# Two tiles of the second chunk run inside the first chunk's tail, and start-up work is spread over other steps

## The chip, the cores and the metric

The kernel runs on one core of one Trainium2 chip. The metric is the device time of one execution in microseconds (us). Three runs gave 989.15, 988.88 and 988.53 us, so the median is 988.88. The engines are named as the profile names them: PE does matrix multiplication (PEld is its weight load), DVE is the vector engine, ACT the scalar engine, POOL is GpSimd, and SP only issues transfers.

## The reference

The input `x` has 8 batches of 3136 rows of 256 numbers. The result is the real part of a two-dimensional Fourier transform of each batch, followed by a layer norm, a two-layer network with a ReLU, and a residual sum.

```python
X = np.fft.fft(x, axis=1); X = np.fft.fft(X, axis=2); x = X.real
mu, var = mean(x), mean((x - mu) ** 2)             # over the last axis, 256
xn = (x - mu) / np.sqrt(var + 1e-06) * g_ln
out = x + np.maximum(xn @ w_ch1, 0.0) @ w_ch2      # 256 -> 1024 -> 256
```

## The kernel before, in words

**Stages.** The transform over 3136 rows is done in two steps. Step 1 (`step1`, pieces `i` 0 to 6 of a batch) is a 64-point transform; its result goes to a buffer in DRAM (`store1`) and comes back in another layout (`relayout`). Step 2 (`step2(m, part)`, 64 pieces) finishes the rows: it makes some 196 tokens per piece in PSUM (part `m`), and copies them out three ways: `f` the full value `ck` (ACT), `h` the value rounded to fp32r `ck_hi` (ACT), `l` the rest `ck_lo` (DVE). A token stands for a row and its mirror row. 256 tokens are a chunk `c`; a piece of step 2 can end one chunk and begin the next. Tiles of `ck`, `ck_hi` and `ck_lo` have three buffers, so chunk 3 takes the buffer of chunk 0.

**The network.** The transform over 256 columns is folded into `w1` at the start. Each chunk has 8 tiles `f` of 128 of the 1024 hidden units. `moe1_a(s)` is 6 matmuls into `ab` (two PSUM buffers), which ACT copies (`asb`) and DVE adds and subtracts (`h`, two instructions); `moe1_b(s)` is the ReLU (`h_hi`, ACT) and the rounding rest (`h_lo`, DVE); `moe2(s)` is 12 matmuls with `w2_hi` and `w2_lo` that add to `acc[c, i]`. `residual(c, i)` makes x itself on PE (`psy`), `residual_e` (ACT) and `residual_y` (DVE) finish it and take its statistics, `std` and `inverse_std` make the factor of the layer norm, and `finish` and `store_out` end the chunk. `psy` of chunk c lies in the PSUM buffers that `acc` of chunk c+1 uses next.

**The order.** Nothing schedules the work on PE, ACT, DVE and POOL: they run it in the order in which it is written. After a prologue the main loop takes one step `s` per tile: `moe1_b(s - 1)`, `moe1_a(s)`, then what `add_late` put at `s`, `moe2(s - 3)`, then what `add` put at `s`. Before the change, step `s` is tile `f = s % 8` of chunk `s // 8`.

**Weights.** They arrive as 64-bit floats and are converted in pieces of 512 columns: `convert_z` (ACT) and `convert_m`, `convert_b` (DVE, two instructions each) take a number apart, `finish_w2` (DVE) joins it, `split_w2` rounds it on ACT (`w2_hi`) and takes the rest on POOL (`w2_lo`). Piece `n` of `w2` serves tiles f = 2n and 2n + 1. `rest_w1` and `rest_w1_copy` give `w1_lo`; its second half serves tiles f = 4 to 7. At the start of step 2 PE runs ten matmuls on zeros (`warm_up`).

Of the kernel before, what the change touches and what calls it, by code (L numbers as in the profile page):

```python
# [32 lines left out]
CW = 256  # L33
# [113 lines left out]
def tile_kernel(ctx: ExitStack, tc: tile.TileContext, x, g_ln, w1, w2, tu, tab, tz, ty, tw, out):  # L147
# [121 lines left out]
    def store1(b, i, eng=nc.sync):  # L269
        s = s1[b][:, 2 * i:2 * i + 2]  # L270
        in_order(eng.dma_start(scratch[b][2 * i:2 * i + 2].rearrange("s p d -> p s d"),
                               s.rearrange("p a h d -> p a (h d)")))
# [11 lines left out]
    def width(c):  # L284
        return MAXW if c == LC else CW

    def first_token(m):
        b, j = divmod(m, 8)
        return b * REG + max(gb[2 * j] - 2, 0)
# [49 lines left out]
    PASSES = ((0, 1), (1, 0), (0, 0))  # L339
    hh = {}  # L340

    def moe1_a(s, passes=((0, 1), (1, 0), (0, 0))):
        c, f = divmod(s, 8)
        w = width(c)
        ch = chunk[c][1:]
        fs = slice(128 * f, 128 * f + 128)
        wt = (w1_hi, w1_lo)
        if w <= CW:
            ab = psum.tile([128, 2, CW], F32, tag="ab", name=f"ab{s}", bufs=2)
            pa, pb = ab[:, 0], ab[:, 1]  # L350
        else:
            pa = psum.tile([128, MAXW], F32, tag="ab", name=f"aa{s}", bufs=2)
            pb = psum.tile([128, MAXW], F32, tag="fft", name=f"bb{s}")
        for j, pt in ((0, pa), (1, pb)):
            for n, (wi, xi) in enumerate(passes):
                nc.tensor.matmul(pt, wt[wi][:, j, fs], ch[xi][:, j, :w],  # L356
                                 start=(n == 0), stop=(n == 2))
        asb = work.tile([128, MAXW], F32, tag="asb", name=f"asb{s}")
        h = hh[s] = work.tile([128, 2 * CW], F32, tag="h", name=f"h{s}", bufs=4)
        m = 2 * CW - w  # L360
        nc.scalar.copy(asb[:, :w], pa)  # L361
        nc.vector.tensor_tensor(out=h[:, :w], in0=asb[:, :w], in1=pb, op=ALU.add)  # L362
        nc.vector.tensor_tensor(out=h[:, w:], in0=asb[:, :m], in1=pb[:, :m], op=ALU.subtract)  # L363
# [21 lines left out]
    def in_order(dma):  # L385

        if main:
            tc.keep_in_program_order(dma)
# [6 lines left out]

    def moe2(s, halves=((0, 0), (0, 1), (1, 0), (1, 1))):

        c, f = divmod(s, 8)
        hs = hh[s]
        ws = (w2_hi, w2_lo)  # L400
        for i, side in halves:
            if f == 0 and side == 0:
                acc[c, i] = psum.tile([128, 2, D], F32, tag=f"acc{c % 2}", name=f"acc{c}_{i}", bufs=2)
            h0 = 256 * i + 128 * side if c == LC else 128 * i + 256 * side
            for n, (wi, xi) in enumerate(PASSES):
                nc.tensor.matmul(acc[c, i][:, side], hs[xi][:, h0:h0 + 128], ws[wi][:, f],  # L406
                                 start=(f == 0 and side == 0 and n == 0),
                                 stop=(f == 7 and n == 2), skip_group_check=True)
# [93 lines left out]
    def convert_a(key, wp):  # L502
        convert_m(key, wp)
        convert_z(key, wp)
# [10 lines left out]
    def convert_m(key, wp):  # L515

        high, e = conv[key] if key in conv else convert_e(key, wp)
        low = wp.bitcast(U32).rearrange("p (n two) -> p n two", two=2)[:, :, 0]  # L520
        m = moving.tile([128, 512], I32, tag="f_hi", name=f"m{key}", bufs=2)
        f = moving.tile([128, 512], F32, tag="f_lo", name=f"f{key}", bufs=2)
        nc.vector.tensor_scalar(out=m, in0=high, scalar1=0xFFFFF, scalar2=0x100000,
                                op0=ALU.bitwise_and, op1=ALU.bitwise_or)
        nc.vector.scalar_tensor_tensor(out=f, in0=low, scalar=2.0 ** -32, in1=m,  # L525
                                       op0=ALU.mult, op1=ALU.add)
        conv[key] = high, e, f

    def convert_z(key, wp):
        high, e = conv[key][:2] if key in conv else convert_e(key, wp)  # L530
        nc.scalar.activation(e, high.bitcast(F32), AF.Copy, scale=2.0 ** -112)
# [13 lines left out]
    w1p, w2p = [], []  # L545
# [9 lines left out]
    def load_w2(n, eng=nc.sync):  # L555
        wp = w1p[n]
        eng.dma_start(wp.rearrange("p (f d) -> p f d", f=2), w2v[:, 2 * n:2 * n + 2])
        w2p.append(wp)

    gws, w2f = {}, []  # L560
# [11 lines left out]
    def transform_w1(k, i):  # L572
        for j in range(2):
            if i == 0:
                psw[k, j] = psum.tile([128, 512], F32, tag=f"acc{k}", name=f"psw{k}{j}", bufs=2)
            nc.tensor.matmul(psw[k, j], tw_s[:, i, j], gws[2 * k + i], start=(i == 0),
                             stop=(i == 1))

    def w1_cols(t, k, j):
        return t[:, j, 512 * k:512 * k + 512]  # L580
# [11 lines left out]
    def rest_w1_copy(k):  # L592
        for j in range(2):
            nc.scalar.copy(w1_cols(w1_lo, k, j), psw.pop((k, j)))  # L594

    def finish_w2(n):
        _, e, f = conv.pop(f"w2_{n}")
        nc.vector.scalar_tensor_tensor(out=f, in0=f, scalar=2.0 ** -20, in1=e, op0=ALU.mult,
                                       op1=ALU.mult)
        return f  # L600

    def split_w2(n, f):
        split(w2_hi[:, 2 * n:2 * n + 2], w2_lo[:, 2 * n:2 * n + 2],
              f.rearrange("p (f d) -> p f d", f=2), nc.gpsimd)
# [6 lines left out]
    def add(s, fn, *args):  # L611

        after.setdefault(s, []).append((fn, args))

    def add_late(s, fn, *args):

        late.setdefault(s, []).append((fn, args))

    first = {}
    for m in range(3, 64):  # L620
        s = 8 * (first_token(m) // CW) - 3
        if s in first:
            second.add(m)
        first.setdefault(s, []).append(m)
    for s, ms in first.items():
        for m in ms:
            add(s, step2, m, "mhf")
        for m in ms:
            add_late(s + 1, step2, m, "l")
    def behind(s):  # L630

        return s + 1 + (len(first[s]) > 1)
# [23 lines left out]
            add(d0, store1, b, i)  # L656
        add(at[-1] + 2, relayout, b)
    for c in range(LC):
        s = 8 * c + (5 if c > 1 else 6)
        add_late(8 * c + 9 + (c < 2), std, c)  # L660
        add_late(8 * c + 10 + (c < 2), inverse_std, c)
        for i in range(2):
            add(s, residual, c, i)
            add_late(s + 1, residual_e, c, i)
            add_late(s + i + 2, residual_y, c, i)
            add_late(8 * c + 11 + i, finish, c, i)
            add(8 * c + 11 + i, store_out, c, i)
    add_late(8 * LC - 2, singles)
    add_late(8 * LC + 7, std, LC)
    add_late(8 * LC, mixed)  # L670
# [15 lines left out]
    with tc.manual_schedule(engines={E.PE, E.Activation, E.DVE, E.Pool}):  # L686
        with tc.manual_schedule(engines={E.SP}):
# [46 lines left out]
            step1_ends(0, 10, NS)  # L734
            store1(0, 5, nc.scalar)
            convert_b("w1_1")
            convert_z("w1_2", w1p[2])
            finish_w1(1)
            step1(0, 6)
            store1(0, 6, nc.gpsimd)  # L740
            load_w2(0, nc.gpsimd)
            nc.gpsimd.dma_start(tab_s[:, :, :gb[4]], tab[:, :, :gb[4]])
            nc.gpsimd.dma_start(tz_s, tz)
# [20 lines left out]
            for i in range(NU):  # L764
# [2 lines left out]
            transform_w1(1, 0)  # L767
            rest_w1(0)
            rest_w1_copy(0)
            transform_w1(1, 1)  # L770
            round_w1(1)
            convert_z("w2_0", w2p[0])
            convert_m("w2_0", w2p[0])
            convert_b("w2_0")
            split_w2(0, finish_w2(0))
            convert_m("w2_1", w2p[1])
            warm_up(10, warm_h)
            step2(0, "m")
            step2(0, "hl")
            step2(1, "m")  # L780
            step2(1, "hl", 0)
            convert_z("w2_1", w2p[1])
            convert_b("w2_1")
            moe1_a(0, ((1, 0), (0, 0), (0, 1)))
            moe1_a(1, ((1, 0), (0, 0), (0, 1)))
            rest_w1(1)
            moe1_b(0)
            step2(0, "f")
            moe1_a(2)
            f = finish_w2(1)  # L790
            moe1_b(1)
            split_w2(1, f)
            moe1_b(2)
            moe1_a(3)
            rest_w1_copy(1)
            step2(1, "f")
            convert_a("w2_2", w2p[2])
            step2(1, "hl", 1)
            moe2(0)
            moe1_b(3)  # L800
            moe1_a(4)
            convert_b("w2_2")
            f = finish_w2(2)
            nc.gpsimd.tensor_scalar(out=neg, in0=ty_s[:, 1, 129:130], scalar1=2.0, scalar2=-1.0,
                                    op0=ALU.mult, op1=ALU.add)
            moe2(1)
            step2(2, "m")
            moe1_b(4)
            split_w2(2, f)
            moe1_a(5)  # L810
            step2(2, "hf")
            step2(2, "l")
            convert_a("w2_3", w2p[3])
            moe2(2)
            add_late(6, convert_b, "w2_3")
            add_late(6, lambda: w2f.append(finish_w2(3)))
            add_late(7, lambda: split_w2(3, w2f.pop()))
            add_late(14, split, t1_hi, t1_lo, tu_s[:, 0:128])

        main.append(True)  # L820
# [34 lines left out]
```

## Time and profile before

| what | value |
|---|---|
| median of three runs | 988.88 us |
| the profiled execution | 988.67 us, span 986.9 us |
| PE busy | 976.8 us (99% of the span) |
| DVE, ACT, POOL busy | 815.5, 535.6, 252.1 us |
| granted TensorE clock | 1.00 throughout |

The span runs from the first to the last instruction of the program; 1.8 us of the execution lie around it. A row of the order of time gives the start in us from the span's start, the duration, engine, line, operation, tiles written and read, and in brackets how long the engine had been idle and who ended that. The views of waits add these up. A line such as L371 is a line of the kernel before; from `moe1_a` on the changed kernel has the same statement 7 to 9 lines further down.

### The profile page before, as it was taken

To read this page: it belongs to the slowest core of one execution; us is meant where nothing else is said; L and a number is where in the kernel's file an instruction comes from. 1 tells how busy PE (TensorE), PEld (TensorE's weight loads), DVE (VectorE), ACT (ScalarE), POOL (GpSimd) and SP (SyncE) were. 2 spreads that over 40 slices of the span, in tenths; PEclk is the share of its full clock that TensorE was granted. 3 is DMA by queue.
4 is the path that set the end of the run, shared out by engine and by line. 5 is a ranking of instruction groups with operands and counts; after the bars stand their busy time and mean duration, and the time that the engine had idled before them with its cause. 6 is when DMAs were issued, how large, how long until landed. Compare 5 with 4: busy or idle time off the path is not lost.

```text
span 986.9 us, 22042 instructions
## 1 busy us (share of the span) xinstructions
PE 976.8 (99%) x8426; PEld 962.9 (98%) x8427; DVE 815.5 (83%) x2190; ACT 535.6 (54%) x1416; POOL 252.1 (26%) x282
## 2 busy tenths in 40 slices
PE   9899999999999999999999999999999999999998
PEld 6699999999999999999999999999999999999998
DVE  6888887888888888878888888888888888888887
ACT  3655655555555555555555556555555554555553
POOL 3247343224322332322342234223322300000000
PEclk9999999999999999999999999999999999999999
DMA  8924352215221252112521242212311112100101
GB/s 336 330 101 134 101 173 76 87 54 150 76 97 55 75 161 87 65 65 73 164 86 54 86 139 87 96 55 75 109 52 36 54 53 88 44 23 22 44 23 44
DMA packets 41161, 92.12 MB, mean 93 GB/s; under 512 B 4080, under 2 KB 18400, under 8 KB 40160
## 3 DMA queue, kind: packets, MB, share of 16 engines
q1 hardware_dynamic: 39088, 87.25, 26.7%
q0 software_dynamic: 736, 2.47, 0.7%
q8 instruction: 67, 1.10, 0.5%
q10 hardware_dynamic: 1232, 0.99, 0.3%
q14 instruction: 38, 0.31, 0.1%
HBM read 50.32 MB, written 40.37 MB: 92 GB/s over the span
## 4 chain that ended last, share of the span: by engine, by line
PE 91%; DVE 7%; ACT 2%; issue 1%; ACTq 0%; DVEq 0%
PE acc L406 50%; PE ab L356 25%; PE ps L311 6%; PE psy L431 4%; PE ps L263 3%; DVE h_lo L371 2%; DVE h L362 1%; DVE h L363 1%; PE pw L683 1%; ACT h_hi L370 1%; DVE ew L538 0%; PE ps L255 0%; PE ps L257 0%; DVE fw L525 0%; DVE st L453 0%
## 5 line engine op out<-in xcount | busy, mean ns | idle before, releaser
L406 PE MATMUL acc<-w_hi,h_lo 128*128 128x256 f32 x1568 | 433.2, 276 | 0.2 <-DVE h_lo L371 0.2
L406 PE MATMUL acc<-w_hi,h_hi 128*128 128x256 f32 x1568 | 433.0, 276 | 0.0
L406 PE MATMUL acc<-w_lo,h_hi 128*128 128x256 f32 x1568 | 433.0, 276 | 0.0
L371 DVE SCALAR_TENSOR_TENSOR h_lo<-h,h_hi 128x512 fp32r<-128x512 f32 x392 | 294.1, 750 | 141.2 <-ACT h_hi L370 138.8
L370 ACT ACTIVATE h_hi<-h 128x512 fp32r<-128x512 f32 x392 | 250.0, 638 | 292.9 <-DVE h L363 292.9
L406 PEld LDWEIGHTS acc<-w_hi,h_lo 128*128 128x128 f32 x1568 | 294.3, 188 | 0.6 <-DVE h_lo L371 0.4
L406 PEld LDWEIGHTS acc<-w_hi,h_hi 128*128 128x128 f32 x1568 | 294.4, 188 | 0.0
L406 PEld LDWEIGHTS acc<-w_lo,h_hi 128*128 128x128 f32 x1568 | 294.4, 188 | 0.0
L356 PE MATMUL ab<-ckl,w_hi 128*128 128x256 f32 x768 | 218.0, 284 | 2.3 <-DVE h L363 2.3
L356 PE MATMUL ab<-ckh,w_lo 128*128 128x256 f32 x768 | 212.7, 277 | 2.0 <-ACT w_lo L594 1.7
L356 PE MATMUL ab<-ckh,w_hi 128*128 128x256 f32 x768 | 212.1, 276 | 0.0
L225 POOL TENSOR_TENSOR fl<-f,fh 128x512 fp32r<-128x512 f32 x49 | 64.0, 1306 | 504.9 <-ACT fh L219 494.2
L362 DVE TENSOR_TENSOR h<-asb,ab 128x256 f32<-128x256 f32 x384 | 158.7, 413 | 0.5 <-ACT asb L361 0.5
L363 DVE TENSOR_TENSOR h<-asb,ab 128x256 f32<-128x256 f32 x384 | 158.9, 414 | 0.0
L356 PEld LDWEIGHTS ab<-ckl,w_hi 128*128 128x128 f32 x768 | 144.2, 188 | 3.5 <-issue 1.9
L356 PEld LDWEIGHTS ab<-ckh,w_lo 128*128 128x128 f32 x768 | 144.3, 188 | 2.5 <-ACT w_lo L594 1.9
L356 PEld LDWEIGHTS ab<-ckh,w_hi 128*128 128x128 f32 x768 | 144.2, 188 | 0.0
L361 ACT COPY asb<-ab 128x256 f32<-128x256 f32 x384 | 137.9, 359 | 8.9 <-PE ab L356 1.2
L267 ACT COPY s<-ps 128x508 f32<-128x508 f32 x56 | 32.8, 586 | 62.6 <-PE ps L263 50.7
L311 PE MATMUL ps<-tab_s,s 112*128 112x98 f32 (+1 forms) x512 | 65.6, 273 | 0.1
L311 PEld LDWEIGHTS ps<-tab_s,s 112*128 112x128 f32 x512 | 61.8, 191 | 0.6 <-PE pw L683 0.6
L332 ACT CAST ckh<-ps 128x392 fp32r<-128x392 f32 (+49 forms) x112 | 39.7, 356 | 39.7 <-PE ps L311 39.5
(111 smaller groups left out, 980.2 us busy)
## 6 DMA issues: line engine op xcount, KB each, us to landing
xs<-x SPq DMA_DIRECT2D x56, 512.0 KB, 4.1
out<-o SPq DMA_DIRECT2D x96, 256.0 KB, 2.0
scratch<-s SPq DMA_DIRECT2D x49, 256.0 KB, 2.3
s<-scratch SPq DMA_DIRECT2D x7, 1792.0 KB, 9.8
w1p_all<-w SPq DMA_DIRECT2D x6, 512.0 KB, 8.9
scratch<-s POOLq DMA_DIRECT2D x4, 256.0 KB, 6.0
w1p_all<-w POOLq DMA_DIRECT2D x2, 512.0 KB, 5.2
s<-scratch SPq DMA_DIRECT2D x1, 896.0 KB, 10.9
```

Of the source, the lines that this page charges most:

```text
L225: nc.gpsimd.tensor_tensor(out=lo, in0=f, in1=hi.bitcast(F32), op=ALU.subtract)
L267: nc.scalar.copy(s[:, :, :, :127], ps[:, :, :, :127])
L311: nc.tensor.matmul(ps[:, h, k0 - base:k1 - base], s2[b][:KP, g, 128 * h:128 * h + 128], tab_s[:, h, k0:k1], start=(h == 0 and g == 2 * j), ...
L332: nc.scalar.copy(hi, src)
L356: nc.tensor.matmul(pt, wt[wi][:, j, fs], ch[xi][:, j, :w], start=(n == 0), stop=(n == 2))
L361: nc.scalar.copy(asb[:, :w], pa)
L362: nc.vector.tensor_tensor(out=h[:, :w], in0=asb[:, :w], in1=pb, op=ALU.add)
L363: nc.vector.tensor_tensor(out=h[:, w:], in0=asb[:, :m], in1=pb[:, :m], op=ALU.subtract)
L370: nc.scalar.activation(h_hi, h, AF.Relu)
L371: nc.vector.scalar_tensor_tensor(out=h_lo, in0=h, scalar=0.0, in1=h_hi.bitcast(F32), op0=ALU.max, op1=ALU.subtract)
L406: nc.tensor.matmul(acc[c, i][:, side], hs[xi][:, h0:h0 + 128], ws[wi][:, f], start=(f == 0 and side == 0 and n == 0), stop=(f == 7 and n = ...
L431: nc.tensor.matmul(ps[:, j, :n], ck[:, j], ty_s[:, j, :n], start=(j == 0), stop=True, skip_group_check=True)
```

## The change

It touches the order alone: the same instructions are issued, on the same data, and no buffer is added. Steps 6 and 7 become tiles 0 and 1 of chunk 1, steps 8 and 9 become tiles 6 and 7 of chunk 0. The piece m = 3 of step 2, which fills most of chunk 2 and the first 15 tokens of chunk 3, moves from step 13 to step 7 (its part `l` from 14 to 12). The conversions of `w2` are spread over other places of the prologue and of steps 6 to 9, the second half of `w1_lo` is copied earlier, and `convert_z` of the third piece of `w1` stands behind the copy of the last piece of step 1. What ends chunks 0 and 1 moves with it.

```diff
+    order = [(0, f) for f in range(6)] + [(1, 0), (1, 1), (0, 6), (0, 7)]
+    order += [(1, f) for f in range(2, 8)]
+    def tile_of(s):
+        return order[s] if s < 16 else divmod(s, 8)
     def moe1_a(s, ...):                       # and moe2
-        c, f = divmod(s, 8)
+        c, f = tile_of(s)
...
-        s = 8 * (first_token(m) // CW) - 3
+        s = 7 if m == 3 else 8 * (first_token(m) // CW) - 3
...
-            add_late(s + 1, step2, m, "l")
+            add_late(12 if m == 3 else s + 1, step2, m, "l")
...
-        s = 8 * c + (5 if c > 1 else 6)
-        add_late(8 * c + 9 + (c < 2), std, c)
-        add_late(8 * c + 10 + (c < 2), inverse_std, c)
+        s = (6, 15)[c] if c < 2 else 8 * c + 5
+        end = (13, 19)[c] if c < 2 else 8 * c + 11
+        add_late(end - 1 if c < 2 else end - 2, std, c)
+        add_late(end if c < 2 else end - 1, inverse_std, c)
...
-            add_late(s + i + 2, residual_y, c, i)
-            add_late(8 * c + 11 + i, finish, c, i)
+            add_late(s + 2 + (i if c > 1 else 0), residual_y, c, i)
+            add_late(end + i, finish, c, i)
...
-            convert_z("w1_2", w1p[2])
             finish_w1(1)
             step1(0, 6)
             store1(0, 6, nc.gpsimd)
+            convert_z("w1_2", w1p[2])
...
+            convert_z("w2_0", w2p[0])
             transform_w1(1, 1)
             round_w1(1)
-            convert_z("w2_0", w2p[0])
...
             moe1_b(0)
-            step2(0, "f")
+            f = finish_w2(1)
             moe1_a(2)
-            f = finish_w2(1)
+            rest_w1_copy(1)
             moe1_b(1)
             split_w2(1, f)
+            convert_m("w2_2", w2p[2])
+            moe1_a(3)
+            convert_z("w2_2", w2p[2])
+            convert_b("w2_2")
             moe1_b(2)
-            moe1_a(3)
-            rest_w1_copy(1)
+            step2(0, "f")
+            moe2(0)
             step2(1, "f")
-            convert_a("w2_2", w2p[2])
             step2(1, "hl", 1)
-            moe2(0)
-            moe1_b(3)
             moe1_a(4)
-            convert_b("w2_2")
             f = finish_w2(2)
             moe2(1)
             step2(2, "m")
-            moe1_b(4)
+            step2(2, "hl")
+            moe1_b(3)
             split_w2(2, f)
             moe1_a(5)
-            step2(2, "hf")
-            step2(2, "l")
-            convert_a("w2_3", w2p[3])
+            moe1_b(4)
+            step2(2, "f")
             moe2(2)
-            add_late(6, convert_b, "w2_3")
-            add_late(6, lambda: w2f.append(finish_w2(3)))
-            add_late(7, lambda: split_w2(3, w2f.pop()))
+            add_late(6, convert_a, "w2_3", w2p[3])
+            add_late(7, convert_b, "w2_3")
+            add_late(9, lambda: w2f.append(finish_w2(3)))
+            add_late(9, lambda: split_w2(3, w2f.pop()))
```

Three places of the orders follow. In them `ab9` is the `ab` of step 9, `ckh3` is `ck_hi` of chunk 3, `ps2_3` the PSUM of piece 3 of step 2; the last number of a name only tells buffers apart.

**ACT, where piece 3 of step 2 is copied out.** Before, between steps 13 and 14:

```order
L361 COPY asb13_798<-ab13_791 128x256
L332 CAST ckh2_483<-ps2_3_815 128x2x181
L334 COPY ck2_482<-ps2_3_815 128x2x181
L332 CAST ckh3_823<-ps2_3_815 128x2x15
L334 COPY ck3_822<-ps2_3_815 128x2x15
L370 ACTIVATE h_hi13_832<-h13_799 128x512
L361 COPY asb14_843<-ab14_836 128x256
```

Now, between steps 7 and 9:

```order
L332 CAST ckh2_478<-ps2_3_598 128x2x181
L334 COPY ck2_477<-ps2_3_598 128x2x181
L332 CAST ckh3_606<-ps2_3_598 128x2x15
L334 COPY ck3_605<-ps2_3_598 128x2x15
L377 ACTIVATE h_hi7_610<-h7_574 128x512
L368 COPY asb8_621<-ab8_614 128x256
L377 ACTIVATE h_hi8_656<-h8_622 128x512
L368 COPY asb9_667<-ab9_660 128x256
L549 CAST w2_hi_73<-fw2_3_540 128x512
```

The first write into chunk 3's buffer moved ahead of the ReLU of step 7 and of the copies for steps 8 and 9, which are now tiles 6 and 7 of chunk 0, whose buffer it is.

**PE, at the end of tile 7 of chunk 0 and behind it.** Before, that was step 7; the first `acc1` stood behind step 11:

```order
L356 MATMUL ab11_714<-ckl1_346,w1_hi_76 128x256
L356 MATMUL ab11_714<-ckh1_345,w1_lo_77 128x256
L356 MATMUL ab11_714<-ckh1_345,w1_hi_76 128x256
L406 MATMUL acc1_0_734<-w2_hi_73,h_lo8_640 128x256
L406 MATMUL acc1_0_734<-w2_lo_74,h_hi8_639 128x256
```

Now it stands right behind `ab9`, tile 7 of chunk 0:

```order
L363 MATMUL ab9_660<-ckl0_337,w1_hi_76 128x256
L363 MATMUL ab9_660<-ckh0_336,w1_lo_77 128x256
L363 MATMUL ab9_660<-ckh0_336,w1_hi_76 128x256
L413 MATMUL acc1_0_675<-w2_hi_73,h_lo6_563 128x256
L413 MATMUL acc1_0_675<-w2_lo_74,h_hi6_562 128x256
```

The first sum of chunk 1, which takes over the buffer of `psy0`, moved two steps forward, behind the last reader of chunk 0.

**DVE, at piece 2 of step 2.** Before (`fw` and `mw` are parts of a conversion):

```order
L371 SCALAR_TENSOR_TENSOR h_lo4_486<-h4_457,h_hi4_485 128x512
L362 TENSOR_TENSOR h5_499<-asb5_498,ab5_491 128x256
L363 TENSOR_TENSOR h5_499<-asb5_498,ab5_491 128x256
L336 TENSOR_TENSOR ckl1_346<-ps2_2_477,ckh1_345 128x2x121
L336 TENSOR_TENSOR ckl2_484<-ps2_2_477,ckh2_483 128x2x75
```

Now:

```order
L369 TENSOR_TENSOR h4_455<-asb4_454,ab4_447 128x256
L370 TENSOR_TENSOR h4_455<-asb4_454,ab4_447 128x256
L605 SCALAR_TENSOR_TENSOR fw2_2_405<-fw2_2_405,ew2_2_403 128x512
L336 TENSOR_TENSOR ckl1_347<-ps2_2_472,ckh1_346 128x2x121
L336 TENSOR_TENSOR ckl2_479<-ps2_2_472,ckh2_478 128x2x75
L378 SCALAR_TENSOR_TENSOR h_lo3_485<-h3_416,h_hi3_484 128x512
L369 TENSOR_TENSOR h5_498<-asb5_497,ab5_490 128x256
```

The two `ckl` of this piece moved from behind `h5` to before `h_lo3`, and ACT writes `ckh1` and `ckh2` for them between its other work there.

More of the change, by code (lines that the diff above doesn't have):

```diff
@@ L396, in moe2 @@
     def moe2(s, halves=((0, 0), (0, 1), (1, 0), (1, 1))):
-        c, f = divmod(s, 8)
+        c, f = tile_of(s)
         hs = hh[s]
@@ L664, in tile_kernel @@
             add_late(s + 1, residual_e, c, i)
-            add_late(s + i + 2, residual_y, c, i)
-            add_late(8 * c + 11 + i, finish, c, i)
-            add(8 * c + 11 + i, store_out, c, i)
+            add_late(s + 2 + (i if c > 1 else 0), residual_y, c, i)
+            add_late(end + i, finish, c, i)
+            add(end + i, store_out, c, i)
     add_late(8 * LC - 2, singles)
@@ L775, in tile_kernel @@
             split_w2(0, finish_w2(0))
+            convert_z("w2_1", w2p[1])
             convert_m("w2_1", w2p[1])
@@ L781, in tile_kernel @@
             step2(1, "hl", 0)
-            convert_z("w2_1", w2p[1])
             convert_b("w2_1")
@@ L787, in tile_kernel @@
             moe1_b(0)
-            step2(0, "f")
+            f = finish_w2(1)
             moe1_a(2)
-            f = finish_w2(1)
+            rest_w1_copy(1)
             moe1_b(1)
             split_w2(1, f)
+            convert_m("w2_2", w2p[2])
+            moe1_a(3)
+            convert_z("w2_2", w2p[2])
+            convert_b("w2_2")
             moe1_b(2)
-            moe1_a(3)
-            rest_w1_copy(1)
+            step2(0, "f")
+            moe2(0)
             step2(1, "f")
-            convert_a("w2_2", w2p[2])
             step2(1, "hl", 1)
-            moe2(0)
+            moe1_a(4)
+            f = finish_w2(2)
+            moe2(1)
+            step2(2, "m")
+            step2(2, "hl")
             moe1_b(3)
-            moe1_a(4)
-            convert_b("w2_2")
-            f = finish_w2(2)
+            split_w2(2, f)
+            moe1_a(5)
+            moe1_b(4)
+            step2(2, "f")
             nc.gpsimd.tensor_scalar(out=neg, in0=ty_s[:, 1, 129:130], scalar1=2.0, scalar2=-1.0,
                                     op0=ALU.mult, op1=ALU.add)
-            moe2(1)
-            step2(2, "m")
-            moe1_b(4)
-            split_w2(2, f)
-            moe1_a(5)
-            step2(2, "hf")
-            step2(2, "l")
-            convert_a("w2_3", w2p[3])
             moe2(2)
-            add_late(6, convert_b, "w2_3")
-            add_late(6, lambda: w2f.append(finish_w2(3)))
-            add_late(7, lambda: split_w2(3, w2f.pop()))
+            add_late(6, convert_a, "w2_3", w2p[3])
+            add_late(7, convert_b, "w2_3")
+            add_late(9, lambda: w2f.append(finish_w2(3)))
+            add_late(9, lambda: split_w2(3, w2f.pop()))
             add_late(14, split, t1_hi, t1_lo, tu_s[:, 0:128])
```

## The prediction

> **What bounds the kernel now.** I read the page first, then PE's waits, then the chain of work that ended last, then the order of time between 33 and 83 us on PE, ACT, DVE and POOL.
>
> ```profile
> span 986.9 us, 22042 instructions
> PE 976.8 (99%) x8426; PEld 962.9 (98%) x8427; DVE 815.5 (83%) x2190; ACT 535.6 (54%) x1416; POOL 252.1 (26%) x282
> PE ab L356 <- DVE h L363: 2.3, 6, 0.8
> PE ab L356 <- ACT w_lo L594: 1.7, 1, 1.7
> ```
>
> PE is busy for 99% of the span, and the change leaves its work as it is. So the time can only move by PE's idle time, and the two rows of waits (total, count, longest) hold nearly all of it behind the start: 4.0 us. The chain shows where it lies:
>
> ```profile
> 82.06 0.34 DVE h L363
> 82.53 0.94 PE ab L356 x6
> 83.48 1.36 PE acc L406 x12
> ```
>
> Up to 82 us the chain runs mostly over DVE, from there on PE, tile after tile: 0.68 us for 6 matmuls and 1.36 for 12, which is 0.113 for one. Only what happens before 83 us counts, plus any new wait. On PE it looks like this:
>
> ```profile
> 36.48 0.36 PE L356 MATMUL ab<-ckl,w_hi 128*128 128x256 f32 x1 [0.32 <-DVE h L363]
> ...
> 39.29 0.28 PE L356 MATMUL ab<-ckl,w_hi 128*128 128x256 f32 x1
> 41.25 0.39 PE L356 MATMUL ab<-ckh,w_lo 128*128 128x256 f32 x1 [1.68 <-ACT w_lo L594]
> ...
> 52.03 0.36 PE L356 MATMUL ab<-ckl,w_hi 128*128 128x256 f32 x1 [0.29 <-DVE h L363]
> ...
> 55.09 0.36 PE L356 MATMUL ab<-ckl,w_hi 128*128 128x256 f32 x1 [0.75 <-DVE h L363]
> ...
> 60.07 0.36 PE L356 MATMUL ab<-ckl,w_hi 128*128 128x256 f32 x1 [0.49 <-DVE h L363]
> ...
> 62.60 0.36 PE L356 MATMUL ab<-ckl,w_hi 128*128 128x256 f32 x1 [0.23 <-DVE h L363]
> ```
>
> From 39.29 to 41.25 is 1.96 us where two matmuls in a row take 0.11, so this wait loses 1.85 us, 0.17 more than the idle shown, since ends of pipelined matmuls overlap. I add 0.17 to each wait below.
>
> **What the change can win.** (a) The wait for `w1_lo`. Its copies stood behind ACT's other work:
>
> ```profile
> 37.50 0.37 ACT L361 COPY asb<-ab 128x256 f32<-128x256 f32 x1
> 37.77 0.64 ACT L370 ACTIVATE h_hi<-h 128x512 fp32r<-128x512 f32 x1
> 39.30 0.62 ACT L542 CAST w_hi<-fw 128x512 fp32r<-128x512 f32 x1 [0.89 <-DVE fw L598]
> 39.82 0.62 ACT L370 ACTIVATE h_hi<-h 128x512 fp32r<-128x512 f32 x1
> 40.35 0.35 ACT L361 COPY asb<-ab 128x256 f32<-128x256 f32 x1
> 40.60 1.08 ACT L594 CAST w_lo<-psw 128x512 fp32r<-128x512 f32 x2
> ```
>
> Now they follow `asb2`: 37.87 + 1.08 = 38.95, before PE asks at 39.4. Won: 1.85 us. (b) The wait at 36.48: the conversion of `w2` piece 1 no longer stands behind step 2's copies on ACT, so DVE starts it up to 0.3 us earlier, but `asb0` limits the gain to about 0.15. (c) The four waits from 52.03 to 62.60, where DVE carried the last two conversions and the statistics on top of the tiles: 1.76 shown, 2.4 with the overlap; the conversions now lie elsewhere, and I let all four go. The sixth wait, near 82 us, stays. Together 4.4 us. The `convert_z` moved behind the last piece's copy wins nothing: that copy waited for PE, not for ACT's queue,
>
> ```profile
> 20.71 0.58 ACT L267 COPY s<-ps 128x508 f32<-128x508 f32 x1 [0.33 <-PE ps L257]
> 22.27 0.42 DVE L536 TENSOR_SCALAR ew<-ew 128x512 int32<-128x512 int32 x1
> ```
>
> and the converted piece, ready by 21.29 + 0.6 = 21.9, still meets its reader at 22.27. Step 2's start hangs on PE's warm-up matmuls, whose number is unchanged. The transfers keep their order up to the loop; those of chunk 0's output leave two steps later, and nothing waits for them.
>
> **What it adds.** (d) The largest term is a circle through ACT at steps 7 to 9. ACT's 15-token cast into `ckh3` writes where `ckh0` lies, and tile 7 of chunk 0 reads that until `ab9` is through. ACT does its work strictly in the written order: above, it sat idle for 0.89 us before `w_hi` at 39.30 although the `h` for the ReLU of 39.82 was there at 38.66:
>
> ```profile
> 38.25 0.41 DVE L363 TENSOR_TENSOR h<-asb,ab 128x256 f32<-128x256 f32 x1
> ```
>
> So behind the cast wait `h_hi7` and `asb8`; behind these on DVE `h_lo7`, `h8` and `y0`; and the next matmul of PE after `ab9`, the first of `acc1`, needs the buffer that `y0` still reads. PE has nothing else in its order, so it idles for the whole circle, however early anything else is. The same series ran once in the trace, from a ReLU to `y`:
>
> ```profile
> 54.98 0.63 ACT L370 ACTIVATE h_hi<-h 128x512 fp32r<-128x512 f32 x1 [0.65 <-DVE h L363]
> 55.64 0.83 DVE L371 SCALAR_TENSOR_TENSOR h_lo<-h,h_hi 128x512 fp32r<-128x512 f32 x1 [0.70 <-ACT h_hi L370]
> 56.40 0.41 DVE L362 TENSOR_TENSOR h<-asb,ab 128x256 f32<-128x256 f32 x1
> 56.73 0.41 DVE L363 TENSOR_TENSOR h<-asb,ab 128x256 f32<-128x256 f32 x1
> 57.06 0.28 DVE L445 TENSOR_TENSOR y<-ye,psy 128x129 f32<-128x129 f32 x1
> 57.26 0.27 DVE L446 TENSOR_TENSOR y<-ye,psy 128x128 f32<-128x128 f32 x1
> 57.57 0.43 DVE L453 BATCH_NORM_STATS2 st<-y 128x6 f32<-128x256 f32 x1
> 58.03 0.18 DVE L454 BATCH_NORM_AGGREGATE mv<-st 128x2 f32<-128x6 f32 x1
> ...
> 68.87 0.20 ACT L332 CAST ckh<-ps 128x30 fp32r<-128x30 f32 x1
> 68.94 0.22 ACT L334 COPY ck<-ps 128x30 f32<-128x30 f32 x1
> ```
>
> 54.98 to 57.53 is 2.55 us, less 0.14 that `h_lo` lost there to POOL. The two small copies ahead take 0.29, and from DVE's end to PE's start pass 0.14 (54.95 to 55.09). Idle: 2.8 us, lost 3.0. The second half of `acc1` needs the second `y`, 1.07 us later (statistics, then `y`), against 0.68 of matmuls: 0.4 more with the hand-over. Term: 3.35 us. (e) `w2` piece 3. Its joining now stands on DVE behind that `y`, the rest of the statistics (0.46 + 0.1 + 0.2), `h_lo8` (0.68) and `h9` (0.67), 2.8 us with its own 0.69; then ACT's `w_hi` 0.62 and POOL's `w_lo` 1.27 (rows below). PE has 0.68 + 0.68 + 1.36 + 0.68 us of matmuls until it needs it: 4.7 against 3.4 us, say 1.15 lost. (f) Piece 2 of step 2 now hands over ACT to DVE to ACT to DVE (`ckh1`, `ckl1`, `ckh2`, `ckl2`) ahead of `h_hi3` and `h_lo3`:
>
> ```profile
> 47.83 0.37 ACT L332 CAST ckh<-ps 128x242 fp32r<-128x242 f32 x1
> 48.34 0.31 ACT L332 CAST ckh<-ps 128x150 fp32r<-128x150 f32 x1
> 48.86 0.63 DVE L336 TENSOR_TENSOR ckl<-ps,ckh 128x242 fp32r<-128x242 f32 x2
> 52.99 0.69 DVE L598 SCALAR_TENSOR_TENSOR fw<-fw,ew 128x512 f32<-128x512 f32 x1
> ```
>
> After `h_lo2` DVE now does one `ckl1` (0.31, half of the pair's 0.63), `h4` (0.67, from 56.40 to 57.06), the joining `fw` (0.6) and the other `ckl1` (0.31), 1.9 us, before tile 0 of chunk 1 can start; PE has the 1.36 us of one `moe2`: 0.55 lost. The ReLU `h_hi3` stands behind `ckh2`, which waits for `ckl1`: 0.31 + 0.64 + 0.68 = 1.63 us to the end of `h_lo3`, less the 0.68 of that tile's matmuls and 0.1 of overlap: 0.85 lost. The piece's matmuls wait 0.3 for the `f` copies of piece 0. Term: 1.7. (g) `h_lo1` and `h_lo2`, now behind conversions in DVE's order: 0.2 and 0.15 to 0.75, taken 0.65. (h) DVE against POOL:
>
> ```profile
> 39.18 0.68 DVE L371 SCALAR_TENSOR_TENSOR h_lo<-h,h_hi 128x512 fp32r<-128x512 f32 x1
> 39.99 1.27 POOL L543 TENSOR_TENSOR w_lo<-fw,w_hi 128x512 fp32r<-128x512 f32 x1 [5.54 <-ACT w_hi L542]
> 40.48 1.33 DVE L371 SCALAR_TENSOR_TENSOR h_lo<-h,h_hi 128x512 fp32r<-128x512 f32 x1 [0.61 <-ACT h_hi L370]
> ```
>
> Alone an `h_lo` takes 0.68 us; met by a running POOL instruction it ended 0.55 after that one's end (41.26). The fold work of batch 1 on POOL now follows `w2` piece 3, so it falls on steps 10 to 14. None met gives 0.1 us of lost PE time there, all met 2.0; between these ends I take 1.0, since in the trace both happened. [...]
>
> **Sum.** 3.35 + 1.15 + 1.7 + 0.65 + 1.0 = 7.85 lost, 4.4 won: 3.4 us more than the profiled 988.67 us. Its time is 0.2 us under the median, 988.88, to which I add it: 992.3 us, 0.35% slower.
>
> **Rivals.** A change under 0.2%, 2.0 us, can hardly be told from none here.
> 1. The circle costs what (d) says, but while PE idles DVE and ACT catch up, so that most of (e), (g) and (h) disappears. Against it: DVE stands still in the circle too. At 1.5 to 2.8 us less than forecast: 989.5 to 990.8.
> 2. ACT's waits at its head do not hold PE: PE reaches `acc1` so late, or the cast comes free so early, that (d) and (f) are hidden. Then (e), (g) and (h) stand alone at 2.8, or 1.6 at the lower ends of (g) and (h), against 4.4 won: 986.1 to 987.3, mostly faster. From the point where all new losses together are under 2.4 us the change wins 2.0 or more; (d) alone exceeds that; the order leaves nothing between `ab9` and `acc1`.
> 3. The idle of 2.8 us slows PE's clock. For it speaks nothing in the trace: the clock is 1.00 throughout, with idle up to 1.68 us. No row gives a price; if the two steps behind it, 4.1 us of matmuls, went half as fast, that would add 4: 996. [...]
>
> **How the numbers follow.** Forecast (990.9 to 994.4) 0.75; rival 1 0.14; rival 2 0.06; rival 3 and a full (h) together 0.05. The bounds: (g) and (h) at their lower ends, with half of (e) and a third of (f) missing, leave 5.5 lost and give 990.0; (h) in full, (g) at its upper end and 0.8 of (c) not won give 994.4. That is the range, 990.0 to 994.4. Faster 0.06, within 0.2% 0.14, slower 0.80.
>
> **What would show it.** In the profile after: PE idle of 2.5 to 3 us before an `acc` matmul, ended by DVE's `y`; ACT idle over 2 us before a 30-column `ckh`, ended by PE's `ab`; PE waiting for POOL's `w_lo`; no wait for ACT's `w_lo` (L601); and from some 90 us on the same tiles as before. Wrong would be the forecast if the `y` wait is under 1.5 us, or if the waits before it sum to less than 1 us.

## The result, and the profile after

Six runs of the changed kernel gave a median of 993.97 us (993.64 to 995.76), six of the kernel before 989.01 us (988.28 to 990.12). The ratio is 1.0054 with a 95% interval of 1.0041 to 1.0067: about 5 us slower. The forecast was 992.3 us with a range from 990.0 to 994.4, and 0.80 on slower. The sign and the largest term's mechanism came as written, the size was 1.7 us short, and the forecast's parts miss in both directions. The profiled execution took 993.79 us.

The page of the changed kernel, its span and the busy time of each engine:

```profile
span 992.0 us, 22049 instructions
PE 979.1 (99%) x8427; PEld 964.6 (97%) x8427; DVE 819.2 (83%) x2190; ACT 535.4 (54%) x1416; POOL 250.5 (25%) x282
```

The span grew by 5.1 us. PE's work is the same; that its busy time reads 2.3 us more comes mostly from a stretch in which it ran slowly, shown below. PE's waits after (in all, count, longest), to be held against the two rows of the prediction:

```profile
PE acc L413 <- DVE y L453: 2.8, 1, 2.8
PE acc L413 <- DVE h_lo L378: 1.5, 3, 0.7
...
PE ab L363 <- DVE h L370: 1.0, 3, 0.6
PE psy L438 <- DVE o L489: 0.9, 1, 0.9
...
PE ab L363 <- DVE ckl L336: 0.3, 1, 0.3
```

The wait for ACT's `w_lo` is gone, as forecast. In its place stands the 2.8 us wait for `y`, two kinds of wait for DVE (`h_lo`, `ckl`) that the kernel before did not have here, and a `psy` that waits for DVE, which it did not have either. The predicted wait for POOL's `w_lo` is missing. The order of time on PE, from the last matmul of tile 7 of chunk 0 on:

```profile
55.77 0.28 PE L363 MATMUL ab<-ckh,w_hi 128*128 128x256 f32 x1
58.81 0.36 PE L413 MATMUL acc<-w_hi,h_lo 128*128 128x256 f32 x1 [2.77 <-DVE y L453]
59.00 0.28 PE L413 MATMUL acc<-w_lo,h_hi 128*128 128x256 f32 x1
...
60.21 0.41 PE L413 MATMUL acc<-w_lo,h_hi 128*128 128x256 f32 x1
60.42 0.41 PE L413 MATMUL acc<-w_hi,h_hi 128*128 128x256 f32 x1
...
62.55 0.40 PE L413 MATMUL acc<-w_hi,h_lo 128*128 128x256 f32 x1
62.77 0.30 PE L413 MATMUL acc<-w_lo,h_hi 128*128 128x256 f32 x1
62.91 0.28 PE L413 MATMUL acc<-w_hi,h_hi 128*128 128x256 f32 x1
```

The `acc` matmul starts 3.04 us after the last `ab` one, where 0.11 is usual. Its first followers still take their 0.28 us; from 60.21 to 62.77 the matmuls start 0.21 apart and take 0.41. That is about half speed, 0.21 against 0.11. The table of stretches for the same trace (length, then busy time of PE, PEld, DVE, ACT and POOL, the granted clock, and the transfers) says why:

```profile
50.00:55.70 5.70, 5.70 (x53) 5.70 (x52) 4.03 (x10) 2.71 (x9) 0.56 (x2) 1.00 0.48 192
55.70:58.80 3.10, 0.34 (x4) 0.17 (x3) 1.85 (x6) 1.56 (x5) 0.00 (x0) 1.00 0.00 0
59.30:62.80 3.50, 3.50 (x18) 3.32 (x18) 3.05 (x10) 0.31 (x1) 0.00 (x0) 0.51 0.00 0
62.80:66.00 3.20, 3.20 (x29) 3.20 (x29) 2.02 (x3) 1.37 (x4) 2.81 (x3) 1.00 0.00 0
```

The granted clock is 0.51 for 3.5 us behind the idle, with 18 matmuls in that time, and 1.00 again behind it, with 29 in 3.2 us. The busy share of PE cannot show this: it reads 3.50 of 3.50. The mean clock of all six timed runs is 0.998, which is what one such stretch, 3.5 us at 0.51, makes in 992 us. That figure alone names no place, though: 7 of the 37 single runs of the kernel before that were timed beside the experiments show 0.998 too, and where the clock fell in those is not recorded.

What held PE, on ACT and DVE of the same trace:

```profile
56.08 0.18 ACT L332 CAST ckh<-ps 128x30 fp32r<-128x30 f32 x1 [1.93 <-PE ab L363]
56.16 0.19 ACT L334 COPY ck<-ps 128x30 f32<-128x30 f32 x1
56.23 0.64 ACT L377 ACTIVATE h_hi<-h 128x512 fp32r<-128x512 f32 x1
...
56.91 0.69 DVE L378 SCALAR_TENSOR_TENSOR h_lo<-h,h_hi 128x512 fp32r<-128x512 f32 x1 [2.74 <-ACT h_hi L377]
...
57.85 0.42 DVE L370 TENSOR_TENSOR h<-asb,ab 128x256 f32<-128x256 f32 x1
...
58.38 0.28 DVE L453 TENSOR_TENSOR y<-ye,psy 128x128 f32<-128x128 f32 x1
```

This is the circle. ACT stands for 1.93 us at the 30-column cast, until PE has read the old buffer; the ReLU follows behind it, DVE has by then stood for 2.74 us, and PE starts 0.15 us after the `y`.

To see where the 5.1 us went I took, for every matmul from 33 to 100 us, the time to the start of the next one, less what it takes in an unbroken row (0.113 us; 0.11 in step 2 and 0.115 for `psy`). I call the sum PE's lost time. It is 7.32 us before and 12.76 after: 5.44 more. The network's first `ab` matmul starts 0.34 us earlier after (33.63 against 33.97), which leaves 5.1, the whole difference of the spans. That start lies between 33.55 and 34.37 in the ten traces of this case, so the 0.34 is not laid to the change. By stretch:

| stretch (us) | lost before | lost after |
|---|---|---|
| 33 to 37 | 1.52 | 1.40 |
| 37 to 50 | 2.32 | 3.44 |
| 50 to 58 (after: with the wait that ends at 58.81) | 1.72 | 2.96 |
| 58 to 63 (after: from 58.2) | 1.23 | 1.83 |
| 63 to 100 | 0.52 | 3.13 |

### The profile page after: what moved, and what is told of

It is laid out like the page before. It is cut to its first block, busy times and chain, and to the rows that moved or that the text cites. A ratio compares the mean times of both kernels' runs of the same rounds, so it can differ in the third digit from the quotient of the medians.

```text
span 992.0 us, 22049 instructions
## 1 busy us (share of the span) xinstructions
PE 979.1 (99%) x8427; PEld 964.6 (97%) x8427; DVE 819.2 (83%) x2190; ACT 535.4 (54%) x1416; POOL 250.5 (25%) x282
## 4 chain that ended last, share of the span: by engine, by line
PE 91%; DVE 5%; ACT 1%; issue 1%; DMA 1%; POOL 0%; SPq 0%; ACTq 0%; POOLq 0%; DVEq 0%
PE acc L413 51%; PE ab L363 25%; PE ps L311 6%; PE psy L438 4%; PE ps L263 3%; DVE h_lo L378 2%; ACT h_hi L377 1%; DVE h L369 1%; DVE h L370 1%; DMA s<-scratch 1%; PE pw L691 0%; DMA scratch<-s 0%; DVE st L460 0%; PE ps L257 0%; PE ps L255 0%
```

## The experiments

Theory A says that the circle of term (d) is the largest loss, and that what is behind it, the halved clock with it, follows from it. Its rivals are that the loss lies in the other places of the change: the hand-overs of step 2's piece 2 (term f), or DVE's work. Theory D, formed after runs 1, 2, 4 and 5, says that DVE's queue sets the pace from 34 to 83 us, so that taking away the wait for `w1_lo` (term a) or spreading the conversions (c) wins nothing: the wait comes back at the next thing that DVE delivers. Each kernel was timed beside the kernel before. All eight lie within 1% of it, so it is the intervals of the ratios that tell them apart.

**1. The circle cut (e1_cast_late).** The changed kernel, but the 15 tokens of piece 3 that belong to chunk 3 are copied out at step 10, behind the ReLU and the copies of steps 8 and 9. All else stays.

```diff
-            if "f" in part:
+            if "f" in part and of in (None, c):
...
+            if m == 3:
+                add(s, step2, m, "mhf", 2)
+                add(10, step2, m, "hf", 3)
+                continue
```

> The changed kernel with one thing moved: the 15-token part of piece 3 of step 2 (its cast and copy into chunk 3) is issued at step 10, behind the last reader of chunk 0, the 181-token part stays at step 7. Theory A (the circle through ACT makes PE idle 2.8 us, and that idle alone brings the half clock behind it): ACT's wait of 1.9 us and PE's wait for y fall to 1.0 us or less, the clock stays at 1.00, and the wait for POOL's w_lo that the slow matmuls hid comes up with 0.9 us. Against the changed kernel's 994.0 us: 2.0 less idle, 1.7 less half clock, 1.2 more for w_lo and the second y: 991.5 us, between 990.5 and 992.3. Rival B (the clock falls for another reason, such as the order of work or the start-up): the half clock stays and the time is 992.8 us or more. Rival C (the time lies in the conversions and hand-overs before step 6): within 0.5 us of 994.0.

Measured: 992.15 us (991.15 to 993.01, 8 runs), ratio 1.0028 (1.0018 to 1.0039); the clock was 1.00 in all eight. Two rows of PE:

```profile
57.19 0.36 PE L413 MATMUL acc<-w_hi,h_lo 128*128 128x256 f32 x1 [0.56 <-DVE y L453]
...
62.89 0.38 PE L413 MATMUL acc<-w_lo,h_hi 128*128 128x256 f32 x1 [0.88 <-POOL w_lo L550]
```

The wait for `y` fell from 2.77 to 0.56 us, the half clock went with it, and the wait for POOL's `w_lo` that the prediction had as term (e) appeared: 0.88 shown, 1.04 lost. Lost time fell by 2.03, to 10.73. So the cast, standing in ACT's order ahead of the ReLU and the copies, makes the circle. Cutting it gives back 1.8 us by the medians and 2.6 by the ratios, not the 4.7 that the gap (2.93) and the slow stretch (1.75) lost, since other work was late behind them; 0.72 us is still lost before the first `acc1`.

**2. PE kept busy in the gap (e2_fill12).** The changed kernel with 12 matmuls on zeros in front of the first `acc1`.

```diff
+            if s == 9:
+                pw = psum.tile([128, 2 * D], F32, tag="y", name="pw9")
+                for i in range(12):
+                    nc.tensor.matmul(pw, warm_h[:, :128], warm_h, start=True, stop=True)
```

> The changed kernel with 12 matmuls of zeros, 2.6 us of PE, put between ab9 and the first matmul of acc1, into a PSUM buffer that is free there. The circle stays as long as it is, but PE works through it. Theory A: the clock stays at 1.00; 1.7 us of half clock are won, of which the wait for POOL's w_lo (0.9 us shown) and the second y (0.2) take back 1.2: 993.4 us, between 992.8 and 994.0, and the profile shows the slow matmuls gone. Rival B (the half clock isn't due to idle PE time): the half clock stays and the time is 994.0 us, with the fill hidden in the wait.

Measured: 994.48 us (993.9 to 999.45, 6 runs), ratio 1.006 (1.0042 to 1.0077). In its trace:

```profile
56.81 2.54 PE L839 MATMUL pw<-warm_h 128*128 128x512 bf16 x11
59.50 0.36 PE L413 MATMUL acc<-w_hi,h_lo 128*128 128x256 f32 x1 [0.16 <-DVE y L453]
```

The added matmuls (11 of the 12 are in the trace) fill the gap, PE's matmuls behind it start 0.11 apart and the clock is 1.00, as in five of the six timed runs; the sixth, 999.45 us, has 0.996. With 0.16 us of idle shown in place of 2.77, the profiled run has 1.00 in place of 0.51, and the circle was left as it was: in this place it is the idle that brings the half clock. The time did not fall, against the expectation. The 1.75 us that the slow stretch lost came back: 1.04 as the wait for `w_lo`, 0.27 at the second `y`, and 0.44 in waits for `h` from 69 to 74 us that lose 0.94 now and 0.50 in the changed kernel. Another 0.7 lies ahead of all this, where the first `ab` matmul started at 34.33 instead of 33.63. Net of what it hides, no cost of the half clock can be seen here.

**3. A shorter fill (e8_fill4).** The same with four matmuls.

> As the kernel with 12 matmuls of zeros ahead of acc1, with 4 (0.87 us): PE's idle there is 1.9 us shown instead of 2.8 (half clock, changed kernel) and 0.2 (no half clock). If the clock falls from some share of idle near 3 us on, it stays at 1.00 as with 12 and the time is that of 12 fills, 994.3 us, within 0.7. If 1.9 us is already enough, the windows show a clock near 0.5 for 3.4 us behind the gap, and a time like the changed kernel's, 994.2. The clock decides, the times can't.

Measured: 994.6 us (994.21 to 995.67, 5 runs), ratio 1.006 (1.0048 to 1.0072). Rows of PE:

```profile
59.26 0.36 PE L413 MATMUL acc<-w_hi,h_lo 128*128 128x256 f32 x1 [1.88 <-DVE y L453]
64.96 0.38 PE L413 MATMUL acc<-w_lo,h_hi 128*128 128x256 f32 x1 [0.77 <-POOL w_lo L550]
```

With 1.88 us idle left, the profiled run kept a clock of 1.00, as four of the five timed runs did in the mean (the other shows 0.998). Again there is no gain: full clock only means an earlier arrival at the wait for `w_lo`.

**4. Piece 3 of step 2 back at step 13 (e3_step2_13).**

```diff
-        s = 7 if m == 3 else 8 * (first_token(m) // CW) - 3
+        s = 8 * (first_token(m) // CW) - 3
...
-            add_late(12 if m == 3 else s + 1, step2, m, "l")
+            add_late(s + 1, step2, m, "l")
```

> The changed kernel with piece 3 of step 2 back at step 13, its rest at 14, as before; all else as changed. Theory A: the circle is gone, but y0 still ends PE's wait before acc1, since PE has 0.9 us less work ahead of it: 1.7 us shown; the clock stays at 1.00; the wait for w_lo comes up. 994.0 less 1.1, less 1.7, plus 1.2: 992.4 us, between 991.0 and 993.2. Rival C: 993.5 or more. If the early piece were a gain by itself the time would be above 994.

Measured: 992.61 us (991.49 to 993.71, 5 runs), ratio 1.0033 (1.0021 to 1.0045). Its waits of PE:

```profile
PE acc L413 <- POOL w_lo L550: 0.9, 1, 0.9
PE acc L413 <- DVE y L453: 0.9, 1, 0.9
```

Undoing the move frees the circle as cutting it did, with 0.9 us shown at `y` (1.02 lost; 1.7 was expected). The mean clock is 1.00 in four of the five runs and 0.998 in one. Two different edits that both take the cast away from this place give the same within their intervals, 1.0028 and 1.0033.

**5. Piece 2's copies in the old order (e4_hl_back).** The changed kernel, but the copies of piece 2 stand together behind `moe1_b(4)`, as before the change. This tests term (f), the hand-overs that the new order pays.

```diff
-            step2(2, "hl")
...
-            step2(2, "f")
+            step2(2, "hf")
+            step2(2, "l")
```

> The changed kernel with piece 2 of step 2 copied out as before, all of ACT's four copies first and DVE's two rests behind moe1_b(4). If term (f) of the prediction, the hand-overs between ACT and DVE, is a plain loss, its undoing wins up to 1.7 us: 992.3. By the order of work it is the lesser evil: tile 0 of chunk 1 then needs its ckl1 behind h5 and h_lo4 on DVE, and PE waits some 2.9 us there instead of 0.3 and 0.6: 995.5 us, and if idle time alone brings the half clock, a second stretch of half clock of 3.4 us behind it, 997 us.

Measured: 997.28 us (996.01 to 998.24, 4 runs), ratio 1.008 (1.0066 to 1.0093). Two rows of PE:

```profile
49.49 0.58 PE L363 MATMUL ab<-ckl,w_hi 128*128 128x256 f32 x1 [2.85 <-DVE ckl L336]
...
62.54 0.41 PE L413 MATMUL acc<-w_hi,h_lo 128*128 128x256 f32 x1 [2.76 <-DVE y L453]
```

And its stretches behind these waits:

```profile
49.50:53.00 3.50, 3.50 (x18) 3.50 (x19) 2.02 (x6) 1.53 (x3) 0.00 (x0) 0.58 1.04 411
53.00:62.50 9.50, 6.77 (x60) 6.58 (x58) 4.73 (x12) 3.63 (x13) 0.90 (x2) 1.00 0.14 56
62.60:66.50 3.90, 3.90 (x21) 3.90 (x22) 3.44 (x11) 0.61 (x3) 0.00 (x0) 0.56 0.00 0
```

Tile 0 of chunk 1 now runs at step 6 and needs `ckl1` that early; with the old order it waits 2.85 us. So the hand-overs of (f) are the smaller loss, 1.2 us in place of 3.0, and not the rival cause. Each of the two idle times is followed by a stretch at about half clock (0.58 and 0.56), and the mean clock of all four runs is 0.996 to 0.998.

**6. Only the tile order (e6_tiles_only).** The kernel before with the new order of tiles and ends, but neither the conversions nor piece 3 moved.

```diff
-        c, f = divmod(s, 8)
+        c, f = tile_of(s)
...
-        s = 8 * c + (5 if c > 1 else 6)
+        s = (6, 15)[c] if c < 2 else 8 * c + 5
+        end = (13, 19)[c] if c < 2 else 8 * c + 11
...
```

> The kernel before with the new order of the first 16 tiles alone, and what ends chunks 0 and 1 at the places that this order needs; conversions, w1_lo and pieces 2 and 3 of step 2 as before. Theory A: without the early cast into chunk 3 there is no circle; PE waits for w1_lo as before (1.7), 2.7 us for ckl1, which tile 0 of chunk 1 needs before DVE has reached it, 0.8 for y0 and 0.6 for the buffer of psy1, instead of the four waits from 52 to 63 us (2.4 lost): 1.7 us above before, and 1.7 more if an idle stretch of 2.7 us brings the half clock each time: 992.7 us. Without the half clock 991.0. Rival C (the order of tiles is harmless by itself): within 0.6 us of before.

Measured: 991.85 us (991.07 to 993.33, 5 runs), ratio 1.0033 (1.002 to 1.0046), between the two times expected. A row of PE, and the stretch behind it:

```profile
49.42 0.39 PE L363 MATMUL ab<-ckl,w_hi 128*128 128x256 f32 x1 [2.70 <-DVE ckl L336]
```

```profile
49.50:53.00 3.50, 3.50 (x30) 3.50 (x31) 3.36 (x8) 1.51 (x3) 0.00 (x0) 1.00 1.03 412
```

The new order costs 3 us by itself. Its largest loss is the `ckl1` that comes too late for it (2.87 lost); 1.36 are lost at the two `y` and 0.52 at a `psy`, and the waits of term (c) are gone. In the profiled run 2.70 us of idle did not lower the clock, where 2.77 and 2.85 did above. Four of its five timed runs have a mean clock of 0.998; where in them the clock fell is not seen, and three of the 23 runs of the kernel before in that session also have 0.998, so this is no more than a hint that the same gap can go either way.

**7. The wait for `w1_lo` alone (e5_w1lo_early).** The kernel before with the copies of the second half of `w1_lo` right behind `moe1_a(2)`. Term (a) counts 1.85 us for this.

```diff
             moe1_a(2)
+            rest_w1_copy(1)
...
-            rest_w1_copy(1)
```

> The kernel before with one thing moved: rest_w1_copy(1), the two copies of the second half of w1_lo, stands right behind moe1_a(2), as in the changed kernel. Term (a) of the prediction books the wait of 1.7 us (1.85 lost) as won: 989.3 less 1.85 gives 987.4 us. Theory D (from 34 to 83 us DVE's queue is the bound, so a wait of PE for another engine is only time in which DVE catches up): the wait goes and comes back as waits for DVE's h at steps 4, 5 and 6, 0.6, 0.5 and 0.7 us, and the time is 989.3, between 988.7 and 989.9.

Measured: 989.32 us (988.21 to 992.68, 12 runs) against 988.87, ratio 1.0007 (0.9999 to 1.0015): no gain. How little room DVE has there is seen in a stretch of the kernel before (DVE is the third busy time, ACT the fourth):

```profile
36.50:63.00 26.50, 23.06 (x187) 22.11 (x188) 23.41 (x53) 15.83 (x41) 9.72 (x12) 1.00 0.64 226
```

In the trace of this run the wait of 1.68 is gone, and these stand on PE:

```profile
45.10 0.36 PE L356 MATMUL ab<-ckl,w_hi 128*128 128x256 f32 x1 [0.39 <-DVE h L363]
48.59 0.36 PE L356 MATMUL ab<-ckl,w_hi 128*128 128x256 f32 x1 [0.25 <-ACT ck L334]
51.77 0.36 PE L356 MATMUL ab<-ckl,w_hi 128*128 128x256 f32 x1 [0.87 <-DVE h L363]
54.82 0.36 PE L356 MATMUL ab<-ckl,w_hi 128*128 128x256 f32 x1 [0.70 <-DVE h L363]
```

Lost time is 7.33 us, against 7.32 before. PE comes to the next tiles 1.85 us earlier and waits there for DVE instead: the sum moved, and did not shrink.

**8. Only the conversions (e7_conv_only).** The changed kernel with the old tile order, ends and place of piece 3, and the last joining of `w2` at step 7. By the terms (a) to (c) this should be the winning half of the change.

```diff
-        return order[s] if s < 16 else divmod(s, 8)
+        return divmod(s, 8)
...
-            add_late(9, lambda: w2f.append(finish_w2(3)))
-            add_late(9, lambda: split_w2(3, w2f.pop()))
+            add_late(7, lambda: w2f.append(finish_w2(3)))
+            add_late(7, lambda: split_w2(3, w2f.pop()))
```

> The changed kernel with the old order of tiles, of chunk ends and of piece 3 of step 2; the conversions, w1_lo and piece 2 of step 2 stand as changed, but w2 piece 3 is joined and rounded at step 7, since tile 6 comes two steps earlier. Theory D: the wait for w1_lo is gone, but DVE has the same work, so it comes back as waits for h3, h_lo2 and h_lo3 (0.4, 0.9, 1.3 us lost) and as 2.1 us for w2 piece 3: 990.7 us, between 989.7 and 991.5. By the prediction's terms (a), (b) and (c) alone, 4.4 won against 2.35 of (f) and (g), it is 987.3.

Measured: 990.02 us (989.34 to 991.43, 11 runs), ratio 1.0013 (1.0004 to 1.0021), a little slower, where the terms give 987.3. Three rows of PE:

```profile
44.20 0.38 PE L413 MATMUL acc<-w_hi,h_lo 128*128 128x256 f32 x1 [0.70 <-DVE h_lo L378]
47.70 0.38 PE L413 MATMUL acc<-w_hi,h_lo 128*128 128x256 f32 x1 [1.17 <-DVE h_lo L378]
...
56.87 0.38 PE L413 MATMUL acc<-w_lo,h_hi 128*128 128x256 f32 x1 [0.97 <-POOL w_lo L550]
```

The wait of (a) is gone, of the 2.41 us of (c) 0.60 are left, and others stand in their place; lost time is 7.72 us. Theory D holds for both halves of the test. None of the eight kernels was faster than the one before.

## Why the prediction was right, and where its steps failed

What each term lost or won in the trace after, in the lost time defined above:

| term | forecast | in the trace after |
|---|---|---|
| (a) `w1_lo` | 1.85 won | gone: 1.84 won |
| (b) wait at 36.48 | 0.15 won | 0.59 to 0.47: 0.12 won |
| (c) four waits, 52 to 63 us | 2.4 won | gone: 2.41 won |
| sixth wait, near 82 us | stays | stays and grows, 0.34 to 0.77: 0.43 lost |
| (d) circle | 3.0 and 0.4 lost | 2.93; the second half 0.22, in the row on the clock |
| (e) POOL's `w_lo` | 1.15 lost | 0 |
| (f) hand-overs | 1.7 lost | 0.44 + 0.77 = 1.21 |
| (g) `h_lo1`, `h_lo2` | 0.65 lost | 0.19 + 0.36 + 0.87 = 1.42 |
| (h) steps 10 to 14 | 1.0 lost | 0.25 + 0.25 = 0.50, at steps 14 and 15 |
| `psy` of chunk 1 | no term | 1.07 lost |
| clock | 0 | 1.75 lost |

Lost are 9.31 and won 4.37, which makes 4.94; the missing 0.5 of the 5.44 are gaps of 0.11 that follow such waits.

- **The circle (d)** came as worked out: 2.77 us idle against 2.8, ended by DVE's `y`, with ACT idle before the 30-column cast (1.93 us, where it had named over 2). Runs 1 and 4 show the cause by two different edits. Without the early cast 0.72 (run 1), 1.02 (run 4) and 1.09 us (run 6) are still lost before the first `acc1`, which the new order puts right behind `ab9`; the circle's own part of the 2.93 is thus about 1.8 to 2.2. Rival 2, that ACT's waits do not hold PE, is out. Rival 1, that the other losses mostly vanish while PE idles, is out by run 2: with the circle as long and the clock up, (e) still lost 1.04 and (h) 0.94.
- **The clock.** Rival 3, given at most 0.05, happened: 2.77 us of idle were followed by a clock of 0.51. The step that failed goes from idle of up to 1.68 us, which had passed at 1.00 in the trace before, to 2.8, which no run had shown. The size failed too: the 4 us of that rival supposed 4.1 us of matmuls at half speed, an assumption that no run shows; there were 18 matmuls, 2.0 us of work, in a stretch of 3.5. The stretch lost 1.75 us, the second half of (d) included, and hid most of what was late behind it.
- **Term (e)** was hidden by exactly that. The forecast gave PE 3.4 us of matmuls until it needs `w_lo`; at half clock these took longer, and the wait vanished. Wherever the clock stayed up with the `w2` piece joined at step 9 (runs 1 to 4) it stood there: 1.04 lost in run 1, against 1.15 forecast.
- **Term (g)** was sized too small. DVE's `mw` was not 0.42 us long but 1.52, as the same operation shows twice in the order of time of the changed kernel, and the `h_lo` and `h` behind it came late:

```profile
39.51 1.30 POOL L550 TENSOR_TENSOR w_lo<-fw,w_hi 128x512 fp32r<-128x512 f32 x1 [7.72 <-ACT w_hi L549]
...
39.57 1.52 DVE L530 TENSOR_SCALAR mw<-w1p_all 128x512 int32<-128x512 int32 x1
...
50.62 0.42 DVE L530 TENSOR_SCALAR mw<-w1p_all 128x512 int32<-128x512 int32 x1
```

The forecast let only the `h_lo` meet POOL. The conversion moved to the place where POOL works on `w_lo`, and pays 1.1 us there. Run 8 bears it out: this `mw` takes 1.53 us there too, at the same place, and 0.41 in the kernel before, which has it at 42.40, where no `w_lo` runs.

- **Term (h)** has its mechanism: four `h_lo` in a row met POOL and took 1.35, 1.19, 1.07 and 1.03 us, where the one ahead of them, at 60.51, took 0.68; two of them are shown.

```profile
63.67 1.35 DVE L378 SCALAR_TENSOR_TENSOR h_lo<-h,h_hi 128x512 fp32r<-128x512 f32 x1 [1.22 <-ACT h_hi L377]
...
66.39 1.19 DVE L378 SCALAR_TENSOR_TENSOR h_lo<-h,h_hi 128x512 fp32r<-128x512 f32 x1 [0.70 <-ACT h_hi L377]
```

PE lost 0.50 to it in the changed kernel, where the slow stretch hid a part, and 0.94 in run 2 with the clock up, against 1.0 forecast.

- **A hand-over without a term.** Behind these steps stand two waits that the sum doesn't have. First the changed kernel, then the same two places before:

```profile
77.52 0.71 PE L438 MATMUL psy<-ty_s,ck 128*128 128x129 f32 x4 [0.91 <-DVE o L489]
...
87.70 0.36 PE L363 MATMUL ab<-ckl,w_hi 128*128 128x256 f32 x1 [0.60 <-DVE h L370]
```

```profile
69.73 1.05 PE L431 MATMUL psy<-ty_s,ck 128*128 128x129 f32 x8
...
82.53 0.36 PE L356 MATMUL ab<-ckl,w_hi 128*128 128x256 f32 x1 [0.18 <-DVE h L363]
```

The `psy` of chunk 1 takes the buffer of chunk 0's `acc`, which the `o` of `finish` reads. Before, the last `finish` of chunk 0 stood at step 12 and this `psy` at the end of step 14, in one row and without a wait; now they stand at 14 and 15. The step that failed is that the prediction followed the moved chunk ends only to `y` and `acc1`, and put nothing here. The wait comes with the new order and its ends: run 6 has 0.52 of it, and the kernel before, run 7 and run 8, with the old order, have none. The wait at 87.70 is the one of the same tile that the forecast let stay: 0.34 lost before, 0.24 in run 6, 0.34 in run 8, 0.77 now, so neither half of the change alone lengthens it. How much of the rest POOL's work owns, which runs beside DVE there, no run separates.

- **Terms (a) to (c)** were right in the table and wrong as a gain. Runs 7 and 8 show that these waits are one lateness of DVE that moves on when its place is taken away. The forecast booked 4.4 us as won and booked the return in other terms, at 0.65 for (g) and a part of (f) and (h). The return in (g) was larger; with the halved clock and the `psy` that is what the forecast of 992.3 lacks to 994.0. That the time stayed in the range is partly luck: (e), (h), (f) and the second half of (d) erred the other way.

The sum of the misses: clock 1.75, `psy` 1.07, (g) 0.77, small gaps 0.5 and the sixth wait 0.43 too little; (e) 1.15, (h) 0.5, (f) 0.5 and the second half of (d) 0.4 too much. That leaves 2.0 too little, of which the earlier start gave 0.34 back. Open is how much of 994.0 the clock owns: cutting the circle removes gap and slow stretch together, and filling the gap removes the stretch at no gain.

## What to carry to other kernels

Before a step is moved forward, look in an engine's written order for a write that must wait for the last reader of the old buffer, and count everything behind that write on its engine: 15 tokens held ACT, DVE and PE in one circle here. Do the same for every buffer whose last reader the change moves: the `psy` that nobody had followed cost 1.07 us. A wait counts as won only if the engine that delivers next has time to spare; with DVE about nine tenths busy (23.4 of 26.5 us) it came back a tile later. Look at the granted clock behind idle times as long as those here (2.76 to 2.85 us were followed by 0.51 to 0.58, 2.70 by 1.00), since PE's busy share shows nothing of it (3.50 of 3.50 us at 0.51).

## What the runs showed of the hardware

An idle time of 2.77 us on PE was followed, 0.5 us after work had begun again, by about 3.4 us with matmuls 0.21 us apart instead of 0.11; the granted clock is 0.51 over the 3.5 us that hold them. In run 5 idle times of 2.85 and 2.76 us did the same, there from the first matmul on, with 0.58 and 0.56 over stretches of 3.5 and 3.9 us. Idle of 2.70 us in run 6 and of 1.88 in run 3 passed at 1.00 in the profiled runs. Why the delay differs, and what sets the length, no run here shows.

A TENSOR_SCALAR on integers with one input took 1.52 us instead of 0.42 beside a POOL instruction that ran from 39.51 to 40.81: it ended 0.28 after that one. In the kernel before an instruction of DVE, an `fw` of the conversions, began first, at 32.62 against 32.99, and took 0.69 us, as all eight of its line (L525) do in that kernel; there POOL's `w_lo` took 1.46 us instead of 1.27 to 1.29.
